# Layer 2's gate and value projections of token blocks 0 and 1 with seven products for eight, weight sums on GpSimd

## The chip, the cores and the metric

One Trainium2 chip (trn2), one of its cores. The time is device microseconds of one execution; before the change three runs gave 792.69 us in the median (792.22 to 793.52). The engines are TensorE (PE in the profile, its weight loads PEld), VectorE (DVE), ScalarE (ACT), GpSimd (POOL) and SyncE (SP), which issues nearly all DMAs.

## What is computed

Attention within clusters, then two feed-forward layers on 1536 tokens of width 512, all in fp32. Layer 2, where the change lies:

```python
def _moe2_ref(x, w_gate, w_val, w_out, rms_g):      # x: 1536 x 512, w_gate and w_val: 512 x 1536
    rms = np.sqrt(np.mean(x * x, axis=-1, keepdims=True) + 1e-06)
    xn = x / rms * rms_g
    g = xn @ w_gate
    silu = g * (1.0 / (1.0 + np.exp(-g)))
    val = xn @ w_val
    return (silu * val @ w_out)                      # w_out: 1536 x 512
```

## The kernel before

Attention takes the first 230 us or so. Then come layer 1 and layer 2, built of *units* that run one behind the other on TensorE. Tokens are cut into three blocks of 512 (BLK, NB), weights into slices of 128 hidden columns (m). Each fp32 matrix product is made of three fast matmuls: every operand is held as a high and a low part (XH and XL of x, w[:, 0] and w[:, 1] of a slice), and high x high, high x low and low x high are summed in PSUM. proj (L578) makes one 128x512 projection with 4 x 3 = 12 matmuls (L583). h_unit (L586) of layer 2 makes gate and value of one slice and one block, 24 matmuls. gate then takes a sigmoid on ScalarE (L601), two products on VectorE (L605, L606) and a rounded copy on ScalarE (L608), and low takes the low part on VectorE (L612). y_unit (L616) multiplies a group of three slices (GROUPS2) with w_out for 128 tokens, 9 matmuls (L631 to L633). Its result is copied into Y by ScalarE for the first group (L646) and added by VectorE for the others (L648).

Weights arrive by DMA in a packed form (w_load, L509) and are converted slice by slice in conv_ops (L524): six steps on VectorE (L530, L532, L536, L542, L544, L546) and one on ScalarE (L534). A converted slice takes one of NPLACES places in SBUF. units() writes out the order of the units. drain (L657) puts the evictions of the last unit on VectorE and ScalarE ahead of a unit's matmuls, and as many conversion steps as unit() finds due from fixed costs per unit (pace). need() forces a slice's conversion where the next unit wants it, room() holds it back while places are short. So the instruction lists of all engines are fixed in advance, and each engine works through its own in order.

Between the layers the rows of Y are normalized (norm_r, norm_y) and transposed on TensorE (turn_unit, L697): ScalarE copies the high parts into XH (L706), VectorE takes the low parts into XL (L709). PSUM has eight banks of 128x512; before, four hold projections (tag h) and four hold y and transposes (tag y). GpSimd adds up attention's exponentials (L395) and rests in both layers.

Of the kernel before, what the change touches and what calls it, by code (L numbers as in the profile page):

```python
# [33 lines left out]
BIG = float(2.0 ** 60)  # L34


@with_exitstack
def clustered_attention_two_ffn(
# [457 lines left out]
    fp = {}  # L496
# [10 lines left out]
    cv = {"loaded": 0, "at": 0, "ops": [], "count": 0, "limit": 6, "soon": NPLACES - 6}  # L507

    def w_load():  # L509
        n = cv["loaded"]  # L510
        layer, i, m = stream[n]
        rows = slice(128 * m, 128 * m + 128)
# [5 lines left out]
        cv["loaded"] += 1  # L518
        cv[n] = (raw[:, :, 1], mid[:, :, 0], t)
# [3 lines left out]

    def conv_ops(n):  # L524

        hi, mid, t = cv.pop(n)
        w = W[stream[n]] = take()
        tf = t.bitcast(F32)

        nc.vector.tensor_scalar(t, hi, 3, 0x3FFFF000, op0=ALU.logical_shift_left, op1=ALU.bitwise_and)  # L530
        yield
        nc.vector.scalar_tensor_tensor(t, hi, 0xC0000000, t, op0=ALU.bitwise_and, op1=ALU.bitwise_or)  # L532
        if pace["on"]:
            nc.scalar.activation(hi.bitcast(F32), hi.bitcast(F32), AF.Square, scale=2.0 ** 15)  # L534
# [7 lines left out]
        nc.vector.scalar_tensor_tensor(w[:, 0], hi.bitcast(F32), 1.125 * 1.125, tf, op0=ALU.is_ge, op1=ALU.mult)  # L542
# [3 lines left out]
        nc.vector.scalar_tensor_tensor(w[:, 1], mid, 2.0 ** -36, tf, op0=ALU.mult, op1=ALU.mult)  # L546
        yield

    def conv(n_ops=1):

        for _ in range(n_ops):
            if not cv["ops"]:
                if cv["at"] >= cv["limit"] or not room():
                    return
                while cv["loaded"] <= cv["at"]:
                    w_load()
                cv["ops"] = [conv_ops(cv["at"])]
                cv["at"] += 1
            next(cv["ops"][0])
            cv["count"] += 1  # L560
            if cv["count"] == 6:
                cv["count"] = 0
                cv["ops"] = []
            while cv["loaded"] < min(cv["limit"], cv["at"] + fp["ahead"]):
                w_load()

    def need(key):
        while key not in W or cv["ops"] and stream[cv["at"] - 1] == key:
            before = cv["at"], cv["count"]
# [577 lines left out]
```

## Time and profile before

| | |
|---|---|
| runs, median of 3 | 792.69 us |
| span of the profiled execution | 789.3 us |
| TensorE busy in the span | 783.0 us |
| VectorE busy in the span | 569.1 us |
| ScalarE busy in the span | 353.4 us |
| GpSimd busy in the span | 167.6 us |
| layer 2, from its first projection (480.6) to the end | 308.7 us |

The span runs from the first to the last instruction of the profiled execution, the only time that its page gives for it; it lies 3.4 us under the median of the runs. A matmul's own record lasts 0.39 us because matmuls overlap; what one costs is the distance to the next, which the chain of waits shows. VectorE's records overlap a little too. Idle time of an engine counts only where the engine that sets the end waits for it.

### The profile page before, as it was taken

The page shows a single profiled execution, that of the slowest core. Times are in us where ns is not written, and L with a number is a line of the kernel's source. Part 1 is how long each engine was busy: PE and PEld are TensorE (multiplying, and loading weights), DVE is VectorE, ACT ScalarE, POOL GpSimd, SP SyncE. Part 2 cuts the span into 40 slices and gives each one's busy share as a digit, 9 for nine tenths or more (in the row PEclk, how much of TensorE's full clock was granted, in tenths as well). Part 3 has the DMA queues.
Part 4 walks back from the last instruction along what each step waited for, and adds up shares of the span by engine and source line. Part 5 has one row for each costly group of instructions (what it writes and reads, how often), then busy time and mean ns, then how long its engine had stood idle before and what let it go on. Part 6 is the DMA issues. An engine that isn't in the chain of part 4 may idle for free.

```text
span 789.3 us, 10670 instructions
## 1 busy us (share of the span) xinstructions
PE 783.0 (99%) x3786; PEld 605.9 (77%) x3786; DVE 569.1 (72%) x1081; ACT 353.4 (45%) x666; POOL 167.6 (21%) x186
## 2 busy tenths in 40 slices
PE   8999999999999999999999999999999999999998
PEld 4666676676568888888888878888888888888887
DVE  6767787776676878777778788988777888733333
ACT  7676676765566555434444435333333222211110
POOL 5878999997000000000000000000000000000000
PEclk9999999999999999999999999999999999999999
DMA  7756675581333555454443520536555544200003
GB/s 201 175 138 171 161 179 123 138 215 38 107 120 106 173 175 165 158 158 150 143 137 130 161 81 27 159 108 196 175 190 187 159 153 149 73 1 1 1 32 129
DMA packets 32677, 103.40 MB, mean 131 GB/s; under 512 B 5016, under 2 KB 5356, under 8 KB 32624
## 3 DMA queue, kind: packets, MB, share of 16 engines
q1 hardware_dynamic: 32612, 102.72, 44.0%
q8 instruction: 30, 0.49, 0.3%
q14 instruction: 23, 0.19, 0.1%
q10 hardware_dynamic: 12, 0.00, 0.0%
HBM read 81.02 MB, written 3.15 MB: 107 GB/s over the span
## 4 chain that ended last, share of the span: by engine, by line
PE 92%; DVE 4%; ACT 3%; issue 0%; ACTq 0%; DVEq 0%
PE h L583 38%; PE y L631 9%; PE y L632 9%; PE y L633 9%; PE pv L403 8%; PE mp L333 5%; PE sc L382 4%; PE sc L383 4%; PE sum L422 1%; DVE a L603 1%; PE simt L168 1%; ACT a L599 1%; ACT a L598 1%; PE xt L701 1%; PE sum L411 1%; PE oht_ps L219 0%
## 5 line engine op out<-in xcount | busy, mean ns | idle before, releaser
L335 DVE TENSOR_REDUCE M<-mp 128x1 f32<-128x384 f32 x186 | 94.5, 551 | 43.8 <-PE mp L333 43.6
L583 PE MATMUL h<-xh,aa 128*128 128x512 f32 x360 | 116.0, 391 | 0.1
L395 POOL TENSOR_TENSOR acc<-acc,P 128x384 f32<-128x384 f32 x112 | 109.3, 1010 | 4.1 <-ACT P L385 3.5
L583 PE MATMUL h<-xh,bb 128*128 128x512 f32 x312 | 100.9, 389 | 0.1
L385 ACT ACTIVATE P<-sc 128x384 f32<-128x384 f32 x192 | 82.4, 490 | 40.1 <-PE sc L383 32.8
L583 PE MATMUL h<-xh,place 128*128 128x512 f32 x288 | 92.7, 389 | 0.0
L534 ACT ACTIVATE raw<-raw 128x512 f32<-128x512 f32 x62 | 42.1, 679 | 107.7 <-DVE bits L532 105.4
L648 DVE TENSOR_TENSOR Y<-y,Y 128x512 f32<-128x512 f32 (+1 forms) x85 | 57.7, 680 | 31.2 <-PE y L633 31.2
L583 PEld LDWEIGHTS h<-xh,aa 128*128 128x128 f32 x360 | 67.6, 188 | 16.0 <-issue 1.2
L403 PE MATMUL pv<-P,v 128*64 128x384 f32 x384 | 70.6, 492 | 0.0
L583 PE MATMUL h<-xl,aa 128*128 128x512 f32 x180 | 70.1, 389 | 0.0
L583 PEld LDWEIGHTS h<-xh,bb 128*128 128x128 f32 x312 | 58.5, 188 | 12.7 <-DVE bb L546 0.6
L382 PE MATMUL sc<-aa,bb 112*128 112x384 f32 x192 | 66.2, 345 | 0.0
L383 PE MATMUL sc<-aa,bb 97*128 97x384 f32 x192 | 65.0, 338 | 0.0
L603 DVE SCALAR_TENSOR_TENSOR a<-h,a 128x512 f32<-128x512 f32 x48 | 33.1, 690 | 41.9 <-ACT a L599 41.7
L583 PEld LDWEIGHTS h<-xh,place 128*128 128x128 f32 x288 | 54.0, 188 | 11.3
L583 PE MATMUL h<-xl,bb 128*128 128x512 f32 x156 | 60.7, 389 | 0.0
L583 PE MATMUL h<-xl,place 128*128 128x512 f32 x144 | 56.0, 389 | 0.0
L333 PE MATMUL mp<-bb,aa 112*128 112x384 f32 x186 | 52.5, 360 | 0.3
L403 PEld LDWEIGHTS pv<-P,v 128*64 128x64 f32 x384 | 25.4, 136 | 31.5 <-issue 30.3
L532 DVE SCALAR_TENSOR_TENSOR bits<-raw,bits 128x512 uint32<-128x512 uint32 x68 | 46.8, 688 | 1.3
L608 ACT CAST bb<-a 128x512 fp32r<-128x512 f32 x34 | 21.1, 622 | 53.2 <-DVE a L606 33.5
(207 smaller groups left out, 1538.4 us busy)
## 6 DMA issues: line engine op xcount, KB each, us to landing
raw<-w_out SPq DMA_DIRECT2D x28, 512.0 KB
mid<-w_out SPq DMA_DIRECT2D x28, 511.8 KB
raw<-w_in SPq DMA_DIRECT2D x16, 512.0 KB
mid<-w_in SPq DMA_DIRECT2D x16, 511.8 KB
raw<-w_gate SPq DMA_DIRECT2D x12, 512.0 KB
raw<-w_val SPq DMA_DIRECT2D x12, 512.0 KB
mid<-w_gate SPq DMA_DIRECT2D x12, 511.8 KB
mid<-w_val SPq DMA_DIRECT2D x12, 511.8 KB
```

Source lines behind the costliest of these rows:

```text
L333: nc.tensor.matmul(mp, A[0:112, h, 0, 128 * qt:128 * qt + 128], Bk[0:112, h, 0, HALF * n:HALF * n + HALF], start=True, stop=True)
L335: nc.vector.tensor_reduce(st["M2", p][:, j, n:n + 1], mp, axis=AX.X, op=ALU.max)
L382: nc.tensor.matmul(sc, Bk[0:112, h, 0, ks], A[0:112, h, 0, qs], start=True, stop=False)
L383: nc.tensor.matmul(sc, Bk[0:97, h, 1, ks], A[0:97, h, 1, qs], start=False, stop=True)
L385: nc.scalar.activation(P, sc, AF.Exp, scale=0.125)
L395: nc.gpsimd.tensor_tensor(acc, acc, P, op=ALU.add)
L403: nc.tensor.matmul(pv[64 * h:64 * h + 64, 0:HALF], st["v", p][:, h, kt], st["P", p, i, h], start=(kt == 0), stop=(kt == NT - 1))
L583: nc.tensor.matmul(h, w[:, wi, fs], x[:, kc, cs], start=(n == 0), stop=(n == 11))
L631: nc.tensor.matmul(y[:, c], g[:, 0, fs], w[:, 0, c], start=(m == m0), stop=False)
L632: nc.tensor.matmul(y[:, c], g[:, 0, fs], w[:, 1, c], start=False, stop=False)
L633: nc.tensor.matmul(y[:, c], g[:, 1, fs], w[:, 0, c], start=False, stop=(m == ms[-1]))
L648: nc.vector.tensor_tensor(Y[:, c], y[:, c], Y[:, c], op=ALU.add)
```

## The change

The two projections of a pair of slices (m, m+1) for blocks 0 and 1 are seen as a 2x2 by 2x2 block product: the weights cut by slice and by halves of the 512 inputs, x by halves and blocks. Seven products of 6 matmuls replace eight (Winograd's form of Strassen's). Three of them take sums of x (fp["xt"], made once by turn_pair at the transposes), three take sums of weights (keys with a negative m in the stream, made by w_sums on GpSimd, split into high and low part by ScalarE, L555, and VectorE, L557). Results are summed partly in PSUM (B is summed on over four products, and copied out by ScalarE after three of them), partly by additions on VectorE (L726) and GpSimd (L735). Block 2 goes as before, in units of its own (one_unit). Groups of layer 2 have two slices instead of three. The conversion's steps are now paced against running totals of TensorE's and VectorE's estimated work, all eight PSUM banks have one tag, and layer 1's groups change their order.

```diff
-GROUPS1 = [3, 4, 3, 3, 3]
-GROUPS2 = [3, 3, 3, 3]
-NPLACES = 26
+GROUPS1 = [3, 3, 4, 3, 3]
+GROUPS2 = [2] * 6
+NPLACES = 24
...
+    def w_sums(i, m, w, f):
...
+        def op(o, x, y, op):
+            fp["gp"].append(lambda: nc.gpsimd.tensor_tensor(o, x, y, op=op))
+
+        for c in (left, right):
+            op(f[:, c], w[:, 0, c].bitcast(F32), w[:, 1, c].bitcast(F32), ALU.add)
+        if m % 2 == 0:
+            fp["f"] = f
+            return
+        f1, f2 = fp.pop("f"), f
+        s, r = (pf.tile([128, 512], F32, tag="s", bufs=3, name=f"s{i}_{m}_{n}") for n in range(2))
+        op(s[:, left], f2[:, left], f2[:, right], ALU.add)
+        op(s[:, right], s[:, left], f1[:, left], ALU.subtract)
+        op(r[:, left], f1[:, left], f2[:, left], ALU.subtract)
+        op(r[:, right], f1[:, right], s[:, right], ALU.subtract)
...
+        if m < 0:
+            while fp["gp"]:
+                fp["gp"].pop(0)()
+            s = fp.pop(("s", i, m))
+            nc.scalar.copy(w[:, 0], s)
+            yield
+            nc.vector.tensor_tensor(w[:, 1], s, w[:, 0].bitcast(F32), op=ALU.subtract)
+            yield
...
+    def product(h, w, c, x, start):
+        n = 0
+        for kc in range(2):
+            fs = slice(c + 128 * kc, c + 128 * kc + 128)
+            for wi, xi in ((0, 0), (0, 1), (1, 0)):
+                nc.tensor.matmul(h, w[:, wi, fs], x[xi][:, kc], start=start and n == 0, stop=(n == 5),
+                                 skip_group_check=not start)
...
+    def four_unit(i, m, part):
...
+        if part == 0:
+            for k in "BA":
+                C[k] = fp["h1"](f"{k}{i}_{m}")
+            product(C["B"], ws[0], 0, x_of(0, 0), True)
+            product(C["A"], ws[0], 256, x_of(2, 0), True)
+        elif part == 1:
+            C["E"] = fp["h1"](f"E{i}_{m}")
+            product(C["B"], ws[0], 256, fp["xt"][0], False)
+            product(C["E"], ws[0], 0, x_of(0, 1), True)
+        elif part == 2:
+            product(C["B"], ws[0], 0, fp["xt"][1], False)
+            product(C["E"], ws[0], 256, x_of(2, 1), False)
+        else:
+            product(C["B"], ws[0], 256, fp["xt"][2], False)
...
+        def keep(k, src):
+            C[k] = pf.tile([128, 512], F32, tag="u", bufs=4, name=f"{k}{i}_{m}")
+            nc.scalar.copy(C[k], c[src])
+
+        def plus(o, x, u):
+            nc.vector.tensor_tensor(o, x, u, op=ALU.add)
+
+        if part == 0:
+            later.append((lambda: (keep("u", "B"), plus(c["A"], c["A"], C["u"]), gated(i, c["A"], m, 0, 0)), None,
+                          lambda: gated(i, c["A"], m, 0, 1)))
+        elif part == 1:
+            later.append((lambda: (keep("v", "B"), keep("e", "E")),))
+        elif part == 2:
+            later.append((lambda: (keep("w", "B"), plus(c["E"], c["E"], c["v"]), gated(i, c["E"], m, 1, 0),
+                                   nc.gpsimd.tensor_tensor(C["w"], C["w"], c["e"], op=ALU.add), gated(i, C["w"], m + 1, 1, 0)), None,
+                          lambda: (gated(i, c["E"], m, 1, 1), gated(i, C["w"], m + 1, 1, 1))))
...
+        def spread(i, m, zs):
+            f, s = fours(i, m), [one(i, m), one(i, m + 1)]
+            return [f[0], zs[0], s[0], f[1], zs[1], zs[2], f[2], s[1], zs[3], f[3], zs[4], zs[5]]
...
-    fp["h"] = lambda layer, name: [psf.tile([128, 512], F32, tag="h", bufs=4, name=f"h{name}_{i}") for i in range(layer)]
-    fp["y"] = lambda name: psf.tile([128, 512], F32, tag="y", bufs=4, name=name)
+    fp["h"] = lambda layer, name: [psf.tile([128, 512], F32, tag="h", bufs=8, name=f"h{name}_{i}") for i in range(layer)]
+    fp["h1"] = fp["y"] = fp["tp"] = lambda name: psf.tile([128, 512], F32, tag="h", bufs=8, name=name)
```

Left out of the diff: gated (L670), which is the old gate and low cut into steps for one projection at a time (sigmoid L673, products L677, copy L681, low part L684), turn_pair (L740: L759 to L772), which makes the three sums of x beside the transposes, and the new accounts in room() and unit(). In the change's own numbering the six conversion steps are L564, L566, L568, L574, L576 and L578, y's matmuls L793 to L795, its addition L810, product's matmul L659 and block 2's L621.

Where instructions stand now, for slices 6 and 7. TensorE before: the gate's 12 matmuls of slice 6 for block 0 end, the value's 12 begin (a row is one or two matmuls, numbers behind the names are buffers).

```order
L583 MATMUL h2_6_0_0_6161<-xh_103,place1_3129 128x512 x2
L583 MATMUL h2_6_0_0_6161<-xl_104,place1_3129 128x512
L583 MATMUL h2_6_0_0_6161<-xh_103,place1_3129 128x512
L583 MATMUL h2_6_0_1_6162<-xh_103,bb1_108 128x512
L583 MATMUL h2_6_0_1_6162<-xl_104,bb1_108 128x512
L583 MATMUL h2_6_0_1_6162<-xh_103,bb1_108 128x512 x2
```

TensorE now, part 1 of the gate's seven products: six more matmuls into B, from sums of x (place5, bb2) and of weights (bb1), then six into E, from x itself and the same weights.

```order
L659 MATMUL B0_6_6284<-place5_3133,bb1_108 128x512
L659 MATMUL B0_6_6284<-bb2_110,bb1_108 128x512
L659 MATMUL B0_6_6284<-place5_3133,bb1_108 128x512 x2
L659 MATMUL B0_6_6284<-bb2_110,bb1_108 128x512
L659 MATMUL B0_6_6284<-place5_3133,bb1_108 128x512
L659 MATMUL E0_6_6343<-xh_103,bb1_108 128x512
L659 MATMUL E0_6_6343<-xl_104,bb1_108 128x512
L659 MATMUL E0_6_6343<-xh_103,bb1_108 128x512 x2
L659 MATMUL E0_6_6343<-xl_104,bb1_108 128x512
L659 MATMUL E0_6_6343<-xh_103,bb1_108 128x512
```

A product has 6 matmuls where a projection had 12, and B goes on where ScalarE has read it. VectorE before, among the y units of slices 3 to 5: products of the gate, a low part, Y additions, and conversion steps between them.

```order
L605 TENSOR_TENSOR a2_5_2_6087<-h2_5_2_0_6060,a2_5_2_6087 128x512
L606 TENSOR_TENSOR a2_5_2_6087<-h2_5_2_1_6061,a2_5_2_6087 128x512
L530 TENSOR_SCALAR bits57_6019<-raw57_6017 128x512
L612 TENSOR_TENSOR place5_3133<-a2_5_2_6087,place5_3133 128x512
L648 TENSOR_TENSOR Y_3125<-y2_1_0_0_6098,Y_3125 128x512
L532 SCALAR_TENSOR_TENSOR bits57_6019<-raw57_6017,bits57_6019 128x512
L536 TENSOR_SCALAR mid57_6018<-mid57_6018 128x512
L648 TENSOR_TENSOR Y_3125<-y2_1_1_0_6113,Y_3125 128x512
```

VectorE now, in the gate's half of slices 6 and 7 (E's addition, products of E, of W, which GpSimd added up, and of block 2, a Y addition, and the two low parts of weight sums).

```order
L726 TENSOR_TENSOR E0_6_6343<-E0_6_6343,v0_6_6357 128x512
L576 TENSOR_SCALAR bits68_6338<-place1_3129 128x512
L677 TENSOR_TENSOR a2_6_1_6412<-E0_6_6343,a2_6_1_6412 128x512
L677 TENSOR_TENSOR a2_7_1_6415<-w0_6_6409,a2_7_1_6415 128x512
L578 SCALAR_TENSOR_TENSOR place1_3129<-mid68_6337,bits68_6338 128x512
L677 TENSOR_TENSOR a2_7_2_6434<-h0_7_2_6419,a2_7_2_6434 128x512
L810 TENSOR_TENSOR Y_3125<-y2_2_3_0_6438,Y_3125 128x512
L557 TENSOR_TENSOR place0_3128<-s1_7_0_6372,place0_3128 128x512
L557 TENSOR_TENSOR bb0_106<-s1_7_1_6373,bb0_106 128x512
```

L726 and L557 are new. The list of such a half, from A0_6's addition to A1_6's, has 27 two-operand instructions and 11 TENSOR_SCALAR, the next half 29 and 7. GpSimd before has nothing in layer 2; now, for the sums of the value's slices 6 and 7 (s1) it has:

```order
L532 TENSOR_TENSOR bits66_6182<-place3_3131 128x256 x2
L532 TENSOR_TENSOR bits67_6281<-bb1_108 128x256 x2
L532 TENSOR_TENSOR s1_7_0_6372<-bits67_6281 128x256
L532 TENSOR_TENSOR s1_7_0_6372<-s1_7_0_6372,bits66_6182 128x256
L532 TENSOR_TENSOR s1_7_1_6373<-bits66_6182,bits67_6281 128x256
L735 TENSOR_TENSOR w0_6_6409<-w0_6_6409,e0_6_6359 128x512
L532 TENSOR_TENSOR s1_7_1_6373<-bits66_6182,s1_7_0_6372 128x256
```

The full weights are put together from high and low part (bits66, bits67), then the sums s1; W's addition for the gate (w0_6) stands among them.

## Rows read from the trace of the kernel before

**Rows 1.** The page, part 1: busy time, share of the span, instructions.
```profile
PE 783.0 (99%) x3786; PEld 605.9 (77%) x3786; DVE 569.1 (72%) x1081; ACT 353.4 (45%) x666; POOL 167.6 (21%) x186
```
**Rows 2.** Busy time by stretches of layer 2; columns as the first line says.
```profile
core 0: us, PE busy (x) PEld busy (x) DVE busy (x) ACT busy (x) POOL busy (x), PEclk, DMA share, GB/s
480.60:520.00 39.40, 39.40 (x192) 33.11 (x191) 35.20 (x69) 17.35 (x35) 0.00 (x0) 1.00 0.26 81
...
600.00:640.00 40.00, 40.00 (x179) 33.10 (x178) 31.07 (x57) 10.52 (x18) 0.00 (x0) 1.00 0.52 169
...
680.00:720.00 40.00, 40.00 (x179) 33.10 (x178) 18.88 (x30) 6.78 (x11) 0.00 (x0) 1.00 0.00 1
```
**Rows 3.** The chain of waits, 472 to 494 us: start, length, what.
```profile
472.43 13.66 PE h L583 x60
486.09 1.75 PE xt L701 x16
...
493.29 0.23 PE y L631
493.52 0.23 PE y L632
```
**Rows 4.** Waits, 480.6 to 690 us: total us, times, longest; the longest of eleven.
```profile
ACT raw L534 <- DVE bits L532: 48.3, 23, 6.0
```
**Rows 5.** Timeline of VectorE, 520 to 528 us: start, length, instruction.
```profile
520.58 0.42 DVE L544 TENSOR_SCALAR bits<-bb 128x512 uint32<-128x512 uint32 x1
521.03 0.69 DVE L546 SCALAR_TENSOR_TENSOR bb<-mid,bits 128x512 fp32r<-128x512 uint32 x1
521.64 0.42 DVE L530 TENSOR_SCALAR bits<-raw 128x512 uint32<-128x512 uint32 x1
...
522.70 0.42 DVE L536 TENSOR_SCALAR mid<-mid 128x512 uint32<-128x512 uint32 x1
523.04 0.68 DVE L612 TENSOR_TENSOR aa<-a,aa 128x512 fp32r<-128x512 f32 x1
...
525.63 0.68 DVE L542 SCALAR_TENSOR_TENSOR aa<-raw,bits 128x512 fp32r<-128x512 f32 x1
526.34 0.43 DVE L544 TENSOR_SCALAR bits<-aa 128x512 uint32<-128x512 uint32 x1
```
**Rows 6.** Groups by line and shape: count, busy us, mean ns, idle before.
```profile
L648 DVE TENSOR_TENSOR Y<-y,Y 128x512 f32<-128x512 f32 x83 | 56.8, 687 | 30.2 <-PE y L633 30.2
L694 DVE SCALAR_TENSOR_TENSOR Y<-Y,rr,gain 128x512 f32<-128x512 f32 x12 | 8.6, 745 | 0.1
L690 DVE TENSOR_TENSOR rt<-rt,ssq 128x4 f32<-128x4 f32 x9 | 1.5, 163 | 0.3
L648 DVE TENSOR_TENSOR Y<-y,Y 128x256 f32<-128x256 f32 x2 | 0.8, 424 | 1.0 <-PE y L633 1.0
...
L608 ACT CAST bb<-a 128x512 fp32r<-128x512 f32 x34 | 21.1, 622 | 53.2 <-DVE a L606 33.5 <-DVE a L603 19.8
```
**Rows 7.** The same view, GpSimd's additions.
```profile
L395 POOL TENSOR_TENSOR acc<-acc,P 128x384 f32<-128x384 f32 x112 | 109.3, 1010 | 4.1 <-ACT P L385 3.5
...
L160 POOL TENSOR_TENSOR xh<-kraw,xh 128x768 fp32r<-128x768 f32 x1 | 1.8, 1837 | 0.0
```
**Rows 8.** Timeline, 65 to 73 and 215 us: VectorE beside GpSimd, and alone.
```profile
65.02 7.74 POOL L395 TENSOR_TENSOR acc<-acc,P 128x384 f32<-128x384 f32 x8
65.49 0.56 DVE L442 TENSOR_TENSOR sum<-sum,pvs 128x384 f32<-128x384 f32 x1
...
215.77 0.55 DVE L442 TENSOR_TENSOR sum<-sum,pvs 128x384 f32<-128x384 f32 x1
```
**Rows 9.** Timeline, 5 to 8 us: GpSimd and VectorE.
```profile
5.20 0.82 POOL L965 CAST aa<-qhl 64x768 fp32r<-64x768 f32 x1 [2.04 <-ACT qhl L156]
...
5.83 1.00 DVE L160 TENSOR_TENSOR qhl<-qraw,qhl 128x768 fp32r<-128x768 f32 x1
6.08 1.45 POOL L261 CAST aa<-qhl 64x768 fp32r<-64x768 f32 x1
```

More of the change, by code (lines that the diff above doesn't have):

```diff
@@ L800, in units, with four, one, fours @@
-        for t in range(4 * NB):
-            yield y(2, len(GROUPS2) - 1, t)
+        def four(i, m, part):
+            gain = (-1, 0, -2, 3) if i else (0, 0, 0, 4)
+            return (lambda: four_unit(i, m, part), 1.36 if part == 3 else 2.72,
+                    ((1.2, 0.0, 1.8, 0.6), (1.8, 0.0, 3.0, 1.2))[i][part], list(four_keys(i, m, part)), gain[part])
+        def one(i, m):
+            return (lambda: one_unit(i, m), 2.72, (0.6, 1.2)[i], [(2, i, m)], -i)
+        def fours(i, m):
+            return [four(i, m, k) for k in range(4)]
@@ new lines, in mix @@
+        def mix(xs, zs):
+            r = []
+            for i, x in enumerate(xs):
+                r += [x] + zs[len(zs) * i // len(xs):len(zs) * (i + 1) // len(xs)]
+            return r
+        yield from [h(1, m, b) for b in range(NB) for m in range(GROUPS1[0])]
+        for m in range(GROUPS1[0]):
+            yield done(1, m)
+        for n in range(1, len(GROUPS1) - 1):
+            m0, g = sum(GROUPS1[:n]), GROUPS1[n]
+            ks = []
+            for m in range(m0, m0 + g):
+                ks += [[h(1, m, b)] for b in range(NB)]
+                ks[-1].append(done(1, m))
+            for b in range(NB):
+                yield from ys(1, n - 1, b)
+                if n == 2 and b == 0:
+                    yield (tables, 0.0, 0.0, [], 0)
+                for k in ks[g * b:g * b + g]:
+                    yield from k
@@ new lines, in units @@
+        n = len(GROUPS1) - 1
+        new = range(sum(GROUPS1[:n]), M1)
+        yield from (*ys(1, n - 1, 0), *hs(1, new, 0), *ys(1, n - 1, 1), *hs(1, new, 1), *ys(1, n, 0))
+        yield from mix(ys(1, n - 1, 2), [norm(0), *scales(0)[:3]])
+        yield from (scale(3), *ys(1, n, 1))
+        hz, yz = hs(1, new, 2), ys(1, n, 2)
+        yield from (hz[0], norm(1), scale(4), scale(5), hz[1], scale(6), pair(0), scale(7), hz[2], pair(1),
+                    *(done(1, m) for m in new), pair(2), pair(3), *yz)
@@ L803, in clustered_attention_two_ffn @@
+        fs, gs, zs = fours(0, 0), fours(1, 0), scales(2)
+        yield from (fs[0], norm(2), zs[0], fs[1], zs[1], zs[2], fs[2], zs[3], turn(8), gs[0], turn(9), gs[1], turn(10), turn(11),
+                    gs[2], one(0, 0), one(0, 1), fs[3], one(1, 0), one(1, 1), gs[3])
+        for j in range(1, len(GROUPS2)):
+            zs = ys(2, j - 1)
+            for i in range(2):
+                yield from spread(i, 2 * j, zs[6 * i:6 * i + 6])
+        yield from ys(2, len(GROUPS2) - 1)
     work = list(units())
@@ L824, in room, with cost, fill, layer_of @@
         return True
-    pace = {"due": 0.0, "on": False, "n": 0}
+    pace = {"on": False, "pe": 0.0, "dve": 0.0, "post": 0.0}
+    def cost():
+        m, n = (stream[cv["at"] - 1][2], cv["left"]) if cv["ops"] else (stream[cv["at"]][2], 6) if cv["at"] < len(stream) else (0, 0)
+        return (0.6 if n == 1 else 0.0) if m < 0 else 0.6 if n % 2 else 0.335
+    def fill():
+        while pace["on"] and pace["dve"] + cost() <= pace["pe"] + SLACK[layer_of()]:
+            if not conv(1):
+                break
+    def layer_of():
+        return int(stream[cv["at"]][0] == 2) if cv["at"] < len(stream) else 1
     def unit():
```

224 lines of the change are left out of this document (138 added, 86 removed).

## Prediction

> **What bounds the kernel now.** I read the page's busy times first: TensorE 99% busy, VectorE 72%, ScalarE 45%, GpSimd 21% [rows 1]. [...] The chain of waits agrees: in layer 2 it runs from matmul to matmul [rows 3]. So time can only be won there by fewer matmuls, and VectorE is the next engine in line: 11 to 22% free while it converts. The eleven kinds of waits from 480 to 690 us are all ScalarE's and VectorE's; the longest is ScalarE's for a conversion step [rows 4]. TensorE has none.
>
> **Fewer matmuls.** 60 projection matmuls in a row take 13.66 us, so 0.2277 us each; a y matmul takes 0.23 and sixteen transposes 1.75, four 0.44 [rows 3]. Per pair of slices and per projection (gate or value), token blocks 0 and 1 took 2 x 2 x 12 = 48 matmuls and now take seven products of 6, 42. There are 6 pairs and 2 projections: 12 x 6 = 72 matmuls, 72 x 0.2277 = **16.4 us off TensorE**. Block 2, the y matmuls (432 of them) and the transposes (12 tiles of 4) keep their numbers. TensorE was saturated, so all of this is on the path, if TensorE stays the bound.
>
> **What the rest pays.** I count half a pair (one projection of two slices: 42 + 24 projection matmuls and six y units of 6), which the change repeats with one pattern: 102 x 0.2277 = 23.2 us of TensorE.
>
> VectorE. The lists of the change have 27 to 29 two-operand instructions and 7 to 11 TENSOR_SCALAR between one A addition and the next, from slice 6 on. Back to back a 128x512 two-operand instruction lasts 0.69 us but the next starts after 0.61 (521.03 to 521.64); behind a TENSOR_SCALAR it starts after 0.34 (522.70 to 523.04) [rows 5]. With 27 and 11 that is 27 x 0.605 + 11 x 0.335 = 20.0 us; with 29 and 7, 19.9. A conversion waits on its own results in three places: 0.45 for 0.335 twice (as at 520.58) and 0.71 for 0.605 once (525.63) [rows 5], so 0.34 us a slice and, with three slices, 1.0 us. About **21.0 us of 23.2**, 91%, where before shows 78% from 600 to 640 us [rows 2]. The new load is 24 subtractions for the low parts of the weight sums, 24 additions of A and E, and 24 more Y additions (six groups of two slices for four of three), at the 0.69 us of the same form [rows 6]. Before slice 4's A addition there are no Y additions on VectorE (group 0 goes by ScalarE), and the halves cost 17 us. From the first A addition (A0_0) to the last (A1_10) I add up 199 us by spacing and 10 to 11 for the dependences, 210 us, against 8.6 + 10 x 23.2 = 241 us of TensorE. So 31 us are free, and VectorE may end this stretch some 5 us late at no cost: with B and E held, five or six of the eight PSUM banks take y and block-2 units of 1.4 to 2.7 us before TensorE wants one back. Room: **36 us**.
>
> GpSimd. It had nothing here, and gets per half eight additions of 128x256 (L532) and one of 128x512 (L735). The rows have 1.010 us for 128x384 and 1.837 for 128x768 [rows 7], 2.15 ns a column; eight in a row take 7.74 us [rows 8], so 0.967 from start to start. Worked out from these: 0.69 us for 256 columns and 1.24 for 512; 8 x 0.69 + 1.24 = 6.8 us a half, and some 70 us in the stretch above (80 and 12 of them). GpSimd is far from full. The question is what these 70 us do to VectorE.
>
> The trace of before has hardly a case. Its GpSimd additions ran beside VectorE instructions with one operand in PSUM, and those did not change: 0.56 us at 65.49 beside GpSimd's additions, 0.55 for the same at 215.77 with GpSimd done [rows 8]. The one overlap with a VectorE instruction that has both operands in SBUF is at 5.83 us [rows 9]: GpSimd's copy took 1.45 us beside it, the same copy 0.82 just before; the VectorE instruction took 1.00 us, where 1.03 ns a column from 0.424 (256) to 0.687 (512) [rows 6] makes 0.95. So they do shut each other out, and there GpSimd paid 0.63 us and VectorE 0.05. Bounds for VectorE's loss: nothing (GpSimd always yields) to the whole 70 us. In the change 12.2 of the 20.0 us of a half touch no PSUM at all (the conversion's six steps, L557, L684, W's product), 61%; 3.7 of these are TENSOR_SCALAR with one SBUF operand, for which no row shows whether they collide, and without them it is 43%. A GpSimd instruction that gets in first holds up VectorE only if the next one is of that kind. I take 0.61 x 70 = **43 us** (0.43 would make 30): the engines would take turns, since GpSimd's bursts come right behind the conversion that feeds them. Then TensorE waits for 43 - 36 = **7 us**.
>
> [...]
>
> ScalarE. Per half 3 squares, 6 sigmoids or casts, 4 copies of products and 2 copies of sums, 15 x about 0.62 us [rows 6] = 9 us of 23.2. Covered in time. But it is now in TensorE's way: B is summed on in place, so three times a half TensorE must wait until ScalarE has copied the partial sum. What hides a copy is the 4.1 us (E product, two y) to 5.5 us (A or E product, y, block 2) of matmuls in between, seven to nine copies long. I cost it at nothing; without cover it is the third rival.
>
> The turn from layer 1 to 2. Transposes come in pairs with ScalarE and VectorE splitting sums of x. Four pairs need 4 x (4 x 0.42 + 0.69 + 0.42) = 11 us of VectorE; with four scalings (0.745 each), three gates (two of 0.69), a normalization (11 of 0.16) and four Y additions that is 23 us by durations, some 20 by spacing [rows 6]. TensorE's work there is as long: three units of 2.73, eight transposes of 0.44 and four y units of 2.05 make 20 us [rows 3]. The first product of layer 2 needs the last pair's low parts. Between nothing and 3 us late; I take 1.5, since 20 against 20 leaves no cover. The changed pacing and groups of layer 1 move instructions there but not their number; TensorE gets no more to do there, and VectorE four subtractions for the first pair's weight sums (2.8 us). Nothing, within 1 us either way.
>
> **Sum**, against this execution's own 789.3 us of span: -16.4 + 7 + 1.5 = -7.9, so 781.4. The median of the runs is 792.7, 3.4 us above that span; I carry these 3.4 over: **784.8 us**.
>
> **Rivals.** One, *GpSimd yields or fits in the gaps*: VectorE loses less than 36 us, TensorE never waits for it: -16.4 + 1.5, **777.8 us**. For it: 39% of VectorE's time is open to GpSimd, which needs 6.8 us of 23.2, and in the one overlap GpSimd paid. Against it: 36 us is only half of GpSimd's time.
> Two, on the other side, *VectorE becomes the bound* between A0_0 and A1_10: it loses the whole 70 us, 210 + 70 - 241 - 5 = 34 us that TensorE waits, -16.4 + 34 + 1.5 = +19, **811.8 us**. It ends slower than before from a loss of 36 + 15 = 51 us, 73% of GpSimd's time. For it: a 91% load leaves no slack to hide in.
> Three, *chains through ScalarE*: its queue stands at W's sigmoid, which waits for L735, behind up to six sums on GpSimd (6 x 0.69 + 1.24 = 5.4 us, as long as the cover). If each of 11 halves lost 2 us there, 22 us: -16.4 + 22 + 1.5, **799.8 us**. Against it: block 2 and y units stand between.
> That the matmuls don't become fewer can be left out: TensorE's list has the 72 fewer.
>
> **How the numbers follow.** Forecast (a loss of 36 to 48 us, ending between 779 and 790) 0.37; rival one 0.30; two 0.20; three 0.09; something else 0.04. Faster by over 0.2% (0.2% is about what a measurement of this kernel can tell from no change): 0.30 + nearly all of 0.37, 0.65. Within 0.2%: the edges of forecast and rival two, 0.07. Slower: most of two, three and the rest, 0.28. The range: 776.5 (rival one with a smooth turn) to 805 (rival three, and rival two at 90% of its loss); it leaves out about 0.15.
>
> **What would show it.** Right: the stretches show VectorE at 95% or more until conversions end, L566, L574 or L578 instructions longer than 0.69 us beside L532, L532 above 0.73, and TensorE gaps of some 7 us in all ended by VectorE. Rival one: VectorE's durations as before, only L532 stretched, TensorE without gaps. Rival two: gaps in every half, on weights (L557, L578). Rival three: gaps before L659 ended by ScalarE copies (L723). Wrong altogether would be a matmul spacing other than 0.228 us or layer 1 ending at another time than before.

## The result: 1.2% slower, and the profile after

The changed kernel takes 801.86 us (median of 4 runs, 799.87 to 803.89) where the kernel before takes 792.46 in the same comparison: a ratio of 1.0121, 95% interval 1.0097 to 1.0144. The forecast was 784.8 us, faster. The profiled execution of after has a span of 802.1 us, 12.8 above that of before; it is the slowest of the four runs (803.89 us), and the medians differ by 9.4. One execution of e11_both, below, ran at a granted clock of 0.66 and took 1090.29 us; its median leaves it out.

The page, part 1, of after (busy time, share, instructions; answers to [rows 1]):
```profile
PE 779.1 (97%) x3711; PEld 597.3 (74%) x3711; DVE 640.2 (80%) x1169; ACT 392.5 (49%) x758; POOL 284.2 (35%) x310
```
Stretches of after, columns as in [rows 2]:
```profile
480.60:520.00 39.40, 34.14 (x156) 27.70 (x155) 31.48 (x70) 26.18 (x61) 13.48 (x19) 0.91 0.04 14
...
680.00:720.00 40.00, 39.00 (x171) 31.62 (x169) 35.76 (x59) 13.37 (x24) 10.23 (x11) 1.00 0.34 109
```
TensorE is no longer gapless. At the turn to layer 2 it is busy 34 of 39 us, part of it at a lower clock (0.91 in the mean of the stretch); later it loses up to 2.7 us in a slice of 40. VectorE is busy 89% of the last slice shown and 88 to 93% of the others from 520 to 760 us, not 95% or more. What TensorE waits for in after from 290 us on (engine, line, releaser: total us, times, longest):
```profile
PE B L659 <- ACT v L723: 6.6, 3, 2.7
PE xt L749 <- DVE xl L765: 2.6, 1, 2.6
PE y L793 <- ACT bb L646: 2.1, 1, 2.1
PE y L793 <- ACT bb L681: 1.9, 1, 1.9
PE B L659 <- ACT u L723: 1.8, 1, 1.8
PE B L659 <- DVE xl L765: 0.9, 1, 0.9
PE y L795 <- DVE bb L684: 0.6, 1, 0.6
```
Nine stalls, 16.5 us. Before had one in the same part:
```profile
PE xt L701 <- DVE Y L694: 0.3, 1, 0.3
```
Those of after lie in three places: 2.1 us in layer 1 (302 us), 7.8 us at the turn and the first output sums of layer 2 (487 to 542 us), and 6.6 us ahead of a B product in the last three pairs (670, 722 and 771 us), each ended by ScalarE's copy of B.

The stretch that the prediction reckoned with, from the first A addition (A0_0) to the last (A1_10), in after:
```profile
505.70:765.60 259.90, 251.73 (x1084) 205.25 (x1083) 233.16 (x370) 99.09 (x176) 90.97 (x91) 0.98 0.36 118
```
It takes 259.9 us. VectorE is busy 233.2 of them and idle 26.7. Most of this idle time stands ahead of the gate's second steps, at the head of VectorE's queue (groups of after, 505 to 765 us; last column: idle before, and its releaser; with the rows of the other tiles the gate's waits come to 21 us):
```profile
L684 DVE TENSOR_TENSOR bb<-a,bb 128x512 fp32r<-128x512 f32 x13 | 9.0, 690 | 5.0 <-ACT bb L681 4.8
L677 DVE TENSOR_TENSOR a<-w,a 128x512 f32<-128x512 f32 x11 | 7.6, 688 | 5.2 <-ACT a L673 3.5 <-POOL w L735 1.6
```

### The profile page after: what moved, and what is told of

It reads as the page before. It is cut to its first block, busy times and chain, and to the rows that moved or that the text cites. A ratio compares the mean times of both kernels' runs of the same rounds, so it can differ in the third digit from the quotient of the medians.

```text
span 802.1 us, 10865 instructions
## 1 busy us (share of the span) xinstructions
PE 779.1 (97%) x3711; PEld 597.3 (74%) x3711; DVE 640.2 (80%) x1169; ACT 392.5 (49%) x758; POOL 284.2 (35%) x310
## 5 line engine op out<-in xcount | busy, mean ns | idle before, releaser
L532 POOL TENSOR_TENSOR bits<-place 128x256 f32<-128x256 f32 x10 | 9.6, 977 | 268.2 <-DVE place L578 268.2
L621 PE MATMUL h<-xh,aa 128*128 128x512 f32 x312 | 99.9, 390 | 0.1
L810 DVE TENSOR_TENSOR Y<-y,Y 128x512 f32<-128x512 f32 (+1 forms) x109 | 72.9, 678 | 21.5 <-PE y L795 21.3
L621 PEld LDWEIGHTS h<-xh,aa 128*128 128x128 f32 x312 | 58.6, 188 | 14.1 <-DVE a L641 0.8
L621 PE MATMUL h<-xh,bb 128*128 128x512 f32 x200 | 65.5, 395 | 0.0
L621 PE MATMUL h<-xl,aa 128*128 128x512 f32 x156 | 60.7, 389 | 0.0
L636 ACT ACTIVATE a<-h,half_b 128x512 f32<-128x512 f32 x48 | 32.8, 683 | 42.0 <-PE h L621 42.0
L566 DVE SCALAR_TENSOR_TENSOR bits<-raw,bits 128x512 uint32<-128x512 uint32 x68 | 51.9, 763 | 1.3
L621 PEld LDWEIGHTS h<-xh,bb 128*128 128x128 f32 x200 | 38.4, 192 | 8.2
L532 POOL TENSOR_TENSOR bits<-bb 128x256 f32<-128x256 f32 x20 | 18.3, 934 | 72.0 <-DVE bb L578 63.1
L334 PEld LDWEIGHTS mp<-bb,aa 112*128 112x128 f32 x186 | 32.3, 189 | 15.5 <-issue 5.5
L621 PE MATMUL h<-xl,bb 128*128 128x512 f32 x100 | 39.5, 395 | 0.0
```

The source lines that it names most:

```text
L334: nc.tensor.matmul(mp, A[0:112, h, 0, 128 * qt:128 * qt + 128], Bk[0:112, h, 0, HALF * n:HALF * n + HALF], start=True, stop=True)
L621: nc.tensor.matmul(h, w[:, wi, fs], x[:, kc, cs], start=(n == 0), stop=(n == 11))
L810: nc.vector.tensor_tensor(Y[:, c], y[:, c], Y[:, c], op=ALU.add)
```

## The experiments

Times are medians, ratios are to the kernel before with 95% intervals. "Stretch" is A0_0 to A1_10 of the profiled execution.

### What slows the pairs

**e1_no_sums**
```diff
-        for c in (left, right):
-            op(f[:, c], w[:, 0, c].bitcast(F32), w[:, 1, c].bitcast(F32), ALU.add)
...
+        fp["s", i, -m], fp["s", i, -m - 1] = f1, f2
+        return
```


> The 96 additions and subtractions of weight slices on GpSimd are left out; the bits tiles stand in for the sums, so layer 2 computes with other weights and its output is not the reference's; every matmul, every conversion on VectorE and ScalarE and every gate operation stays. Theory A (the stretched VectorE instructions made VectorE the bound): the six operations of the conversion chain that the trace of after shows at 0.67 to 1.22 us beside GpSimd fall back to 0.42 to 0.69 us, a half pair on VectorE falls from 25.5 us to 23.2 us, the pace of TensorE; the stalls of TensorE at 541, 670, 722 and 771 us and the drops of the clock behind them go; what stays is the turn to layer 2 (about 5 us of stalls, 3.4 us of lost clock) and the stall at 303 us: 785 to 790 us. Theory B (VectorE's head-of-queue waits for ScalarE's casts and for the product E alone hold it): the instructions get shorter but the half pair stays above 25 us: 797 to 802 us.

787.13 us, 0.9935 (0.992 to 0.995): 14.7 us under after, faster than before. Theory A. The stretch in this kernel:
```profile
504.20:746.80 242.60, 241.85 (x1066) 198.95 (x1066) 215.49 (x370) 99.24 (x176) 15.53 (x11) 0.99 0.39 126
```
Two steps of the conversion in it, 505 to 765 us (groups: count, then busy us and mean ns of one):
```profile
L566 DVE SCALAR_TENSOR_TENSOR bits<-raw,bits 128x512 uint32<-128x512 uint32 x30 | 21.6, 719 | 0.5
L568 DVE TENSOR_SCALAR mid<-mid 128x512 uint32<-128x512 uint32 x30 | 13.1, 436 | 0.0
```
The same two in after:
```profile
L566 DVE SCALAR_TENSOR_TENSOR bits<-raw,bits 128x512 uint32<-128x512 uint32 x30 | 25.7, 857 | 0.5
L568 DVE TENSOR_SCALAR mid<-mid 128x512 uint32<-128x512 uint32 x30 | 20.2, 673 | 0.0
```
VectorE has the same 370 instructions and is busy 215.5 us instead of 233.2. So the sums cost it 17.7 us, and TensorE has its own pace back: 242.6 us, of which it is busy 241.9. The run takes away a second thing too: L735 no longer stands behind sums in GpSimd's queue, and L677's wait for W, 5.2 us in after, is gone. The 14.7 us are collisions and this queue together. A single burst in after shows the collision (timeline, VectorE and then GpSimd: start, length, instruction):
```profile
700.06 0.65 DVE L564 TENSOR_SCALAR bits<-raw 128x512 uint32<-128x512 uint32 x1
700.75 1.12 DVE L566 SCALAR_TENSOR_TENSOR bits<-raw,bits 128x512 uint32<-128x512 uint32 x1
701.79 0.96 DVE L568 TENSOR_SCALAR mid<-mid 128x512 uint32<-128x512 uint32 x1
702.66 1.22 DVE L574 SCALAR_TENSOR_TENSOR aa<-raw,bits 128x512 fp32r<-128x512 f32 x1
703.81 0.69 DVE L726 TENSOR_TENSOR E<-E,v 128x512 f32<-128x512 f32 x1
...
701.39 1.07 POOL L532 TENSOR_TENSOR s<-bits 128x256 f32<-128x256 f32 x1
702.54 0.80 POOL L532 TENSOR_TENSOR s<-s,bits 128x256 f32<-128x256 f32 x1
703.30 1.19 POOL L532 TENSOR_TENSOR s<-bits,bits 128x256 f32<-128x256 f32 x1
```
Four instructions that last 0.42 to 0.69 us alone take 0.65 to 1.22; L726, with an operand in PSUM, keeps its 0.69.

**e2_sums_dve**
```diff
-            fp["gp"].append(lambda: nc.gpsimd.tensor_tensor(o, x, y, op=op))
+            fp["gp"].append(lambda: nc.vector.tensor_tensor(o, x, y, op=op))
```


> The 96 sums of weight slices go from GpSimd to VectorE, with the same operands, at the same places of the program. Theory A (a sum on GpSimd costs VectorE what it stretches): the stretched instructions fall back to their durations alone, which gives some 24 us, and the sums cost 96 x about 0.35 us = 34 us of VectorE; VectorE is the bound of the pair stage, so about 10 us more than after: 805 to 815 us. Theory B (GpSimd's lateness is what hurts, since the sums arrive too late): faster than after, 790 to 798 us.

802.03 us, 1.0131 (1.0107 to 1.0156): the time of after. Neither theory's number; the stretch takes 258.6 us:
```profile
503.60:762.20 258.60, 247.94 (x1078) 202.07 (x1077) 238.40 (x450) 98.61 (x176) 15.04 (x11) 0.99 0.37 118
```
VectorE is busy 22.9 us more than without sums, for 80 of them. On GpSimd they cost it 17.7, and the 5.2 us saved are lost again in waits. To give the sums to GpSimd won nothing.

**e6_late**
```diff
-            for f in fp.pop("after", ()):
-                f()
+            old = fp.pop("after", ())
...
             fill()
+            for f in old:
+                f()
```


> The changed kernel with the second steps of the gate (the multiplication by the sigmoid, the subtraction of ScalarE's cast) issued at the end of the next unit's VectorE work instead of at its head; the same instructions otherwise. Theory A (part of VectorE's lateness is its waiting at the head of its queue for ScalarE, 2 to 3 us a half pair): a half pair falls from 25.5 us towards 23.5 us, the stalls of the second halves at 670, 722 and 771 us shrink, and it gives 5 to 12 us: 790 to 797 us. Theory B (VectorE's busy time is all that counts): 800 to 803 us.

794.66 us, 1.0035 (1.0023 to 1.0047): 7.2 us less than after, theory A. The stretch:
```profile
507.30:759.70 252.40, 247.24 (x1079) 202.83 (x1079) 236.27 (x370) 100.16 (x176) 92.67 (x91) 0.98 0.38 121
```
The two groups that were shown of after:
```profile
L684 DVE TENSOR_TENSOR bb<-a,bb 128x512 fp32r<-128x512 f32 x15 | 11.8, 795 | 0.7 <-ACT bb L681 0.7
...
L677 DVE TENSOR_TENSOR a<-w,a 128x512 f32<-128x512 f32 x11 | 7.5, 682 | 1.1 <-POOL w L735 1.1
```
VectorE's work is 3.1 us more (236.3), since some of the moved L684 seem to meet GpSimd now (795 ns for 690; in after the L684 at 572.77 us, beside a GpSimd sum that started at 572.65, took 1.22 us); its idle time falls from 26.7 to 16.1, and the stretch is 7.5 us shorter. So the time of a half pair on VectorE is work plus waits, and either of them buys time.

How VectorE's lateness reaches TensorE is seen on ScalarE in after (timeline; in brackets the idle time before, and its releaser):
```profile
664.68 0.62 ACT L681 CAST bb<-a 128x512 fp32r<-128x512 f32 x1 [6.17 <-DVE a L677]
...
669.34 0.62 ACT L681 CAST aa<-a 128x512 fp32r<-128x512 f32 x1 [3.47 <-DVE a L677]
669.86 0.58 ACT L723 COPY v<-B 128x512 f32<-128x512 f32 x1
```
ScalarE has nothing to do for 3.5 us, but the copy of B stands behind a cast that waits for VectorE's L677; TensorE, which wants to sum on in B, waits until 670.5.

**e7_wide**
```diff
-        for c in (left, right):
-            op(f[:, c], w[:, 0, c].bitcast(F32), w[:, 1, c].bitcast(F32), ALU.add)
+        op(f, w[:, 0].bitcast(F32), w[:, 1].bitcast(F32), ALU.add)
```


> The changed kernel with the sum of a slice's two parts as one GpSimd addition of 128 x 512 instead of two of 128 x 256; 24 instructions for 48, the other 48 as they are. By the GpSimd rows of after, 1.44 us for one against 2 x 0.9 to 1.1 us, GpSimd is busy 10 us less in layer 2. Theory A (VectorE loses in proportion to GpSimd's busy time, 26 us for some 85): VectorE gains 3 us, all of it seen in the time: 797 to 800 us. Theory B (what counts is how many of VectorE's instructions meet one, not how long): no difference, 801 to 803 us.

807.68 us, 1.0195 (1.0179 to 1.0212): 5.8 us more, a miss of both theories. The stretch:
```profile
503.90:767.90 264.00, 249.81 (x1084) 203.03 (x1083) 241.00 (x371) 98.23 (x176) 82.46 (x71) 0.99 0.35 116
```
The second conversion step, 505 to 765 us (groups; lines one lower than in after where they stand behind the sums):
```profile
L565 DVE SCALAR_TENSOR_TENSOR bits<-raw,bits 128x512 uint32<-128x512 uint32 x29 | 31.5, 1088 | 0.5
```
GpSimd is busy 8.5 us less in the stretch, VectorE 7.8 us more: the step that meets the wide sum goes from 857 to 1088 ns. Less GpSimd time cost VectorE more.

**e3_gate_only**
```diff
-        if layer == 2 and i < 2:
+        if layer == 2 and i == 0:
             w_sums(i, m, w, tf)
...
+                return [one(1, m, 0), zs[0], one(1, m + 1, 0), zs[1], one(1, m, 1), ...
```


> Seven products for the gate projection alone; the value projection of all three token blocks as twelve-matmul units, as in before. 36 matmuls fewer than before instead of 72 (8.2 us of TensorE instead of 16.4), half the sums on GpSimd, half the additions of A and E on VectorE and half the copies of B on ScalarE. Theory A (VectorE, with its idle time at the head of its queue, is 10% over TensorE in after): over a whole pair TensorE has 2 x 23.2 + 2 x 4.1 = 54.6 us and VectorE some 51.2 - 4 x 0.69 - 5 (half of the stretch and of the waits) = 43 us, so VectorE fits, the late stalls go, and the time is 789.3 - 8.2 + 5 to 8 for the turn = 786 to 790 us on the median's scale, faster than before. Theory B (the stalls come with each B copy, whoever bounds): half of the late stalls stay, 793 to 797 us.

798.50 us, 1.0092 (1.0063 to 1.0122). Here block 1's plain value units read, in place of the first half of its activations, the difference that the turn stores there; the instructions are those of plain units. All stalls behind 525 us are gone, as theory A has it, but the time is a little above theory B's: what is lost lies at 302 us and at the turn (stalls of 7.5 us from 487 to 523 us, with two drops of the clock, to 0.91 in the mean of 490 to 500 us and to 0.83 in that of 520 to 530), which the expectation priced too low.

### What the turn costs

**e10_plain_turn**, and **e11_both** with the edit of e1_no_sums as well
```diff
-            nc.scalar.copy(v, p1[:, 0:2])
             nc.scalar.copy(XH[:, :, c0], p0)
-            nc.scalar.copy(XH[:, 2:4, c1], p1[:, 2:4])
-            for o, x, y in ((s[:, 0], v, p0[:, 0:2]), (s[:, 1], p1[:, 2:4], s[:, 0]), ...
+            nc.scalar.copy(XH[:, :, c1], p1)
...
-            product(C["B"], ws[0], 256, fp["xt"][0], False)
+            product(C["B"], ws[0], 256, x_of(2, 1), False)
...
```
The same edit stands at B's two other products, and the casts and GpSimd subtractions that follow the differences go with them.


> The changed kernel with the turn to layer 2 as before had it, in pairs: the transposed token blocks are copied and split into their two parts, and the differences of blocks 0 and 1 are left out; the products over those differences read plain parts of the activations in their place, so the output is not the reference's; every matmul, every sum of weights and every gate operation stays. Theory A (the turn costs some 9 to 12 us, the stalls and the slow stretches between 480 and 520 us): those stalls go, the late ones stay, 791 to 794 us. Theory B (VectorE is behind from the turn on anyway, so what is not lost there is lost in the first halves): 798 to 801 us.

797.59 us, 1.0064 (1.0046 to 1.0081): 4.3 us less than after, just under theory B's 798: the turn costs less than I had written. In the profiled execution A0_0 starts 3.5 us earlier than in after, and the stretch is 2.3 us shorter.

> The changed kernel without the differences of the activations at the turn and without the sums of weights on GpSimd, both left out as in the two runs that leave out one of them, so the output is not the reference's; all matmuls stay. Theory A (the 72 fewer matmuls are worth their full 16.4 us, and these two are all that stands against it): 789.3 - 16.4 = 772.9 us of span plus the stalls at 302 and 540 us, 3 to 5 us, on the median's scale 776 to 780 us. Theory B (a third cost is hidden): 782 us or more.

781.13 us, 0.9861 (0.9844 to 0.9877): 6.0 us under e1_no_sums and 1 us over theory A's range. Its rows are read from a second run.

> Without the differences at the turn and without the sums of weights, both left out as in the run before, so the output is not the reference's. Theory A: the 5 us over 776 us are the stall of layer 1 at 302 us with its drop of the clock (2 to 5 us), the first output sums of layer 2 waiting for block 0's last gate at 535 us (1.4 us), and ScalarE's copy of B at 504 us (about 1 us); no stall behind 545 us. Theory B: stalls behind 545 us remain.

781.55 us, 0.9861 (0.9843 to 0.9879), span 779.0 us. The stretch:
```profile
498.20:740.50 242.30, 240.40 (x1065) 197.90 (x1064) 215.53 (x370) 99.24 (x176) 15.54 (x11) 1.00 0.39 126
```
TensorE's longest waits from 290 us on:
```profile
PE B L659 <- ACT v L723: 1.1, 1, 1.1
PE xt L749 <- DVE xl L757: 0.9, 1, 0.9
PE y L781 <- DVE bb L684: 0.6, 1, 0.6
PE y L779 <- ACT bb L646: 0.4, 1, 0.4
```
Theory A: with two of 0.2, 3.4 us of waits, and the last of them is at 532 us. 789.3 - 16.4 + 3.4 = 776.3; 2.7 us are in no wait that the profile names.

**e5_turn**, **e9_turn**, **e14_spaced**: other orders of the same units at the turn (e9_turn and e14_spaced with the edits of e9b, below). In the second expectation "the run above" is e9b. The order of e5_turn:
```diff
...
-        yield from (hz[0], norm(1), scale(4), scale(5), hz[1], scale(6), pair(0), scale(7), hz[2], pair(1),
-                    *(done(1, m) for m in new), pair(2), pair(3), *yz)
+        yield from (scale(3), yo[0], norm(1), scale(4), yo[1], scale(5), yo[2], scale(6), pair(0), yo[3], scale(7), pair(1),
+                    hz[0], hz[1], pair(2), hz[2], *(done(1, m) for m in new), yz[0], pair(3), *yz[1:])
```


> The changed kernel with the units between layer 1 and layer 2 in another order and nothing else: the four output sums of block 2's older group stand behind the norm of block 1 and beside the first two pair transposes, the other two pairs stand between the last activations and the last output sums, so that some 25 us of TensorE work lie beside the four pairs instead of some 15. Theory A (at the turn VectorE's six subtractions a pair are late): the stalls at 488, 499 and 503 us, 5.3 us, and the drops of the clock there shrink to 1 to 2 us, and the whole gives back 4 to 8 us: 794 to 798 us. Theory B (the stalls move to the first products whatever the order, since VectorE is behind from the norm on): 800 to 803 us.

807.19 us, 1.0185 (1.0162 to 1.0208), 5.3 more than after: the first output sum now stands close behind the activation that it needs and waits 4.3 us for ScalarE's cast.

> As the run above, and also four output sums of block 2's older group between the pair transposes, behind the last activations of layer 1 and not ahead of them, so that no output sum stands right behind the activation that it needs. Theory A: the stall at 488 us goes as well, 2.6 us and a drop of the clock: 782 to 786 us. Theory B: the pairs need VectorE for longer than any cover there is, and what is gained at 488 us is lost at the first product: within 2 us of the run above.

806.80 us, 1.0190 (1.0175 to 1.0205), 13.7 more than e9b. In e14_spaced:
```diff
-                    *(done(1, m) for m in new), pair(2), pair(3), *yz[:3])
+                    *(done(1, m) for m in new), yz[0], pair(2), yz[1], pair(3), yz[2])
```


> The kernel of e9b with the last two pair transposes each behind an output sum of layer 1 instead of side by side. Theory A (the pairs' buffers come free too late only because the pairs stand together): the stalls of 2.6 and 1.0 us at 487 and 493 us go, the one of 2.4 us ahead of the first product grows by at most 1 us: 789 to 791 us, faster than before. Theory B (the chain from the transposes through ScalarE and VectorE sets the first product's time): 792 to 794 us, the stall moved to the first product.

802.90 us, 1.0127 (1.0111 to 1.0143), 9.8 more: the wait for the pairs' buffers is gone, as theory A has it, but an output sum waits 3.9 us for a cast, and the first product 5.6 and 1.5 us instead of 2.4. None of these three orders shortened the turn. VectorE and ScalarE pass each pair back and forth, and each takes 2.93 us there (timeline of after, first subtraction of the last three pairs, the Y additions behind them and the A addition; then ScalarE):
```profile
490.69 0.42 DVE L764 TENSOR_TENSOR t<-v,xt 128x256 f32<-128x256 f32 x1
...
493.62 0.42 DVE L764 TENSOR_TENSOR t<-v,xt 128x256 f32<-128x256 f32 x1 [0.36 <-issue]
...
496.56 0.42 DVE L764 TENSOR_TENSOR t<-v,xt 128x256 f32<-128x256 f32 x1 [0.37 <-issue]
...
499.05 2.47 DVE L810 TENSOR_TENSOR Y<-y,Y 128x512 f32<-128x512 f32 x4
...
505.68 0.69 DVE L726 TENSOR_TENSOR A<-A,u 128x512 f32<-128x512 f32 x1
...
502.83 0.56 ACT L723 COPY u<-B 128x512 f32<-128x512 f32 x1
```
The Y additions wait behind the pairs, ScalarE's norm squares wait for the Y additions, and the copy u that TensorE wants waits behind the squares: that is the stall of 1.8 us at 503 us.

### Repairs

**e4_groups**
```diff
-GROUPS1 = [3, 3, 4, 3, 3]
+GROUPS1 = [3, 4, 3, 3, 3]
```


> After with the groups of layer 1's output sums as before, 3 4 3 3 3 instead of 3 3 4 3 3, and nothing else changed. Theory A: the stall of 2.08 us at 303 us in layer 1 is due to this order (the group of three comes when ScalarE's cast is still queued), it goes with it, and its clock with it: 798 to 800 us. Theory B: it comes from the conversions' pace and stays: 801 to 803 us.

801.66 us, 1.0143 (1.0104 to 1.0181), no difference: theory B. The stall moves to 311 us.

**e8_all**: the edits of e5_turn, e6_late and e7_wide together.

> The three edits together: the other order at the turn, the gate's second steps at the end of the unit, one addition of 128 x 512. If the causes add up (turn 4 to 8 us, waits at the head of VectorE's queue 5 to 12 us, wider additions 3 us): 782 to 790 us, faster than before. If one cover is merely exchanged for another: 793 to 798 us, still slower than before.

799.60 us, 1.0097 (1.0075 to 1.0119): above both. By themselves the edits cost 5.3 us, gave 7.2 and cost 5.8, 3.9 us in all; together they give 2.3, so their effects do not add up.

**e9b**: e6_late, the last output sum of layer 1 moved, and another first group; **e9c** is the same without the first edit below.
```diff
-        yield from (fs[0], norm(2), zs[0], fs[1], zs[1], zs[2], fs[2], ...
+        yield from (fs[0], yz[3], fs[1], norm(2), zs[0], zs[1], fs[2], zs[2], ...
...
             zs = ys(2, j - 1)
+            if j == 1:
+                zs = zs[4:6] + zs[:4] + zs[6:]
```


> The changed kernel with the gate's second steps at the end of the unit, and two moves at the turn: the last output sum of layer 1 stands between the first and the second product of layer 2, as cover for ScalarE's copy of B, and the first output sums of layer 2 are those of block 1, so that block 0's last gate has two units more. Theory A (each stall at the turn is a missing cover of one unit): the stall of 3.0 us at 505 us and the two of 3.4 us at 542 and 544 us go, with two of the drops of the clock; the stall of 2.6 us at 488 us stays: 794.7 - 3 - 3 to 7 = 785 to 789 us, faster than before. Theory B (VectorE is behind over the whole turn, and a unit moved there is missing elsewhere): the stall at 505 us comes back before the first product and the others at the next output sums, 792 to 795 us.

> The changed kernel with the gate's second steps at the end of the unit and the first output sums of layer 2 those of block 1, without the moved output sum of layer 1. Theory A: the stalls of 1.6 and 1.8 us at 542 and 544 us and the drop of the clock behind them go, 4 to 6 us less than 794.7 us: 789 to 791 us. Theory B (VectorE is still behind, and what is not lost at 542 us is lost at the next half): 792 to 794 us.

e9b 793.07 us, 1.0011 (1.0003 to 1.0020); e9c 792.73 us, 1.0006 (0.9994 to 1.0018). The stalls at 542 us are gone in both, but the gain on e6_late is 1.6 and 1.9 us, not the 4 to 6 that the expectation puts on them: theory B's number in both, and the moved output sum adds nothing.

**e12_slack** is e9b with the conversions' allowance in layer 1 at -2.0 us, **e13_spaced** that with the order of e14_spaced, **e15_slack** e9b with -0.35 us:
```diff
-SLACK = 0.0, 0.0
+SLACK = -0.35, 0.0
```


> The kernel of e9b with the planner's allowance for conversions in layer 1 lowered by 2 us, so that VectorE is given its conversion steps 2 us of the planner's clock later. Theory A (at 302 us the gate's VectorE operation stands behind five conversion steps): the stall there goes, 1.6 us and, where the clock drops behind it, 1.7 us more: 789.5 to 792 us, level with before or just under it. Theory B (the conversions are only handed over later in one piece): the same stall elsewhere, 793 us.

> The kernel of e12_slack with the last two pair transposes each behind an output sum of layer 1 instead of side by side. Theory A (the pair's buffers come free too late only because the pairs stand together): the stalls of 2.6 and 1.0 us at 487 and 493 us go, the one ahead of the first product, 2.4 us, grows by at most 1 us: 2 to 3 us less than e12_slack. Theory B (the chain from the transposes through ScalarE and VectorE sets the first product's time): the same time within 1 us, the stall moved to the first product.

907.83 us, 1.1451 (1.1427 to 1.1475), and 913.99 us, 1.1532 (1.1512 to 1.1553): at -2.0 us TensorE waits for conversions (L574, L578) all through layer 1. The dose was too large to tell anything.

> The kernel of e9b with the planner's allowance for conversions in layer 1 lowered by 0.35 us, half a conversion step. Theory A (the gate's VectorE operation at 300 us stands behind five conversion steps that were handed over too early): one step fewer stands ahead of it, and the stall of 1.2 us at 302 us goes: 790 to 792 us. Theory B (a step less is converted in time for the matmuls that need it): stalls of TensorE on VectorE's conversions in layer 1, 794 us or more.

790.95 us, 0.9987 (0.9978 to 0.9995): 10.9 us under after, and the one version with all the work that ends below before, by 0.13%. TensorE's longest waits in it from 290 us on:
```profile
PE xt L749 <- DVE xl L765: 2.6, 1, 2.6
PE B L659 <- DVE xl L765: 2.2, 1, 2.2
PE B L659 <- ACT v L723: 1.9, 2, 1.4
```
The wait for L646 at 302 us is gone, theory A: half a conversion step less ahead of the gate is enough.

## Why the prediction was wrong

Against its own sum, in spans, with e11_again as the middle:

| piece | forecast | measured |
|---|---|---|
| 72 matmuls fewer | -16.4 | -16.4, with 6.1 of small waits and rest: e11_again 779.0 |
| the turn (A0_0 starts at 505.7, in e11_again at 498.2) | +1.5 | +7.5 |
| the stretch (259.9 against 242.3) | +7 | +17.6 |
| the tail behind it (36.5 against 38.5) | 0 | -2.0 |
| sum | -7.9 | +12.8 |

**Fewer matmuls: right.** e11_again ends 10.3 us under the span of before, and all but 2.7 of the rest are waits with names.

**VectorE's room: the step that failed.** I added up VectorE's instructions in the stretch, 210 us, and called the rest free up to TensorE's 241, and 36 us with 5 us of lateness, my estimate of what the PSUM banks allow. The work was nearly right: 215.5 us without the sums. But VectorE is not only busy or free. In this order it also stands at the head of its queue, mostly for ScalarE's sigmoids and casts, and I had read its waits in the kernel before [rows 4] only to say that TensorE has none. In e1_no_sums it is idle for 27.1 of 242.6 us, and only 6.3 us of that are waits for TensorE, which a busier VectorE need not make; 17.9 us are waits for ScalarE (two of VectorE's waits in that stretch: total us, times, longest):
```profile
DVE a L677 <- ACT a L673: 7.5, 12, 1.0
DVE E L726 <- PE E L659: 5.1, 2, 3.0
```
So the room was some 6 us where I had 36, or 31 without the lateness. The sums bring 17.7 us of work, and the waits for ScalarE and GpSimd grow by 3.5 (from 17.9 to 21.4, W's among them): 21 us into a room of 6, and the stretch grows by 17.3, from 242.6 to 259.9. With a room of 36 it would not have grown at all. e1_no_sums takes away the one term (14.7 us of time), e6_late part of the waits (7.2 us).

**GpSimd's collisions: right in kind, mis-sized.** I took 43 us for 70 us of GpSimd; it was 17.7 for 75.4 (91.0 less the 15.5 that are left in e1_no_sums). By my room of 36 us this alone would have made rival one. The share of TENSOR_SCALAR that I left open does collide, L568 most of all: 673 ns in after, 436 without the sums. L726 and the L677 that read a PSUM bank keep 0.68 to 0.69 us in both. In the burst at 700 us, L574 started 0.12 us behind a GpSimd sum and lasted 1.22 us; L726 started 0.51 us behind one and lasted 0.69.

**ScalarE at no cost: wrong, but not as rival three had it.** Four of nine stalls end with a copy of B (8.4 us of 16.5), the sign that I gave for that rival, whose 799.8 us were nearest. ScalarE stood at casts that wait for VectorE's L677, though, not at W's sigmoid behind L735 (that wait shows on VectorE, 5.2 us); without the sums the three of 6.6 us are gone.

**The turn: 1.5 us forecast.** By medians it is 4.3 (e10_plain_turn) to 6.0 us (e11_both against e1_no_sums). I set 20 us of VectorE against 20 of TensorE; what I left out is the order in which pairs, Y additions, squares and copies wait for each other. **Layer 1: nothing forecast**, a stall of 2.1 us, since the new pacing hands VectorE five conversion steps ahead of a gate; e15_slack shows it.

That 801.86 us lies inside my range, 776.5 to 805, is luck: its upper part was made of rival three's chain and of 90% of rival two's loss, and the loss was 17.7 of 70 us.

Left open: the 2.7 us in e11_again, why e9_turn loses as much as 13.7 us, and how e1_no_sums' gain divides between collisions and L735's queue, for which no run removes one without the other.

## What to carry to other kernels

An engine's room in a stretch is the stretch less its work and less its waits, in the new order, for all engines but the one whose pace it is to keep; a busy share of 90% (VectorE's 233.2 of 259.9 us in after) was already the bound here. Work given to GpSimd is not free for VectorE: here 80 sums cost it 17.7 us there and 22.9 us on VectorE itself, and in the one comparison made (e7_wide) two short GpSimd instructions cost less than one long one (VectorE busy 233.2 us with the short ones, 241.0 with the long). Where TensorE sums on in a bank that ScalarE must copy first, everything ahead of that copy in ScalarE's queue, and what that waits for, is on TensorE's path: in after 8.4 us of waits.

## What the runs showed of the hardware

At or behind a stall TensorE's granted clock often fell to 0.50: five times in after from 290 us to the tail, the fourth from 671.36 to 674.77 us, where a matmul starts 0.43 us behind the one before (671.66 to 672.09) instead of 0.23. It does not always: here after, then e4_groups at the same place (columns as above; the clock is the third figure from the end):
```profile
668.00:671.00 3.00, 0.50 (x2) 0.46 (x3) 2.96 (x6) 1.66 (x4) 1.30 (x2) 1.00 0.56 177
671.36:674.77 3.41, 3.41 (x10) 2.64 (x9) 3.41 (x6) 0.74 (x2) 2.64 (x3) 0.50 0.85 263
```
```profile
664.00:667.00 3.00, 0.63 (x3) 0.19 (x1) 2.97 (x6) 0.80 (x2) 1.93 (x2) 1.00 0.53 175
667.40:670.80 3.40, 3.40 (x15) 2.81 (x16) 3.40 (x7) 1.56 (x3) 1.81 (x3) 1.00 0.69 208
```
And in the one pair of traces that can be compared it cost nothing where VectorE sets the pace. The last seven A additions (durations, first and last start) in after, with two such drops between them, in e4_groups with none, and in e1_no_sums:
```profile
L726 DVE TENSOR_TENSOR A<-A,u x7: 686/692/693, 613.0 to 765.6; 128x512 f32<-128x512 f32 x7
```
```profile
L726 DVE TENSOR_TENSOR A<-A,u x7: 689/691/693, 609.9 to 762.5; 128x512 f32<-128x512 f32 x7
```
```profile
L726 DVE TENSOR_TENSOR A<-A,u x7: 687/692/700, 606.8 to 746.8; 128x512 f32<-128x512 f32 x7
```
152.6 us with the drops and 152.6 without; 140.0, or 23.3 a half pair, where VectorE is not the bound.
